# Four instead of five of sixteen chunk pairs multiplied in plain f32, with two elementwise steps moved to GpSimd

## The chip, the cores and the metric

The kernel runs on one core of one Trainium2 chip. The metric is the device time of one execution in microseconds (us). Of the three runs of the kernel before, the median is 2019.92 us (2019.54 to 2020.2).

## The reference

An attention through 49 agent tokens is followed by a two-layer network with the activation h - tanh(h). All tensors are float32; q, k and the agents are drawn eight times larger than in the function shown.

```python
B, N, C, n_agents, d_ff = 4, 12480, 128, 49, 2048
def sm(a, b):                                   # softmax of the scaled scores
    s = (a @ b.transpose(0, 2, 1)) / sqrt(C)
    e = exp(s - s.max(-1, keepdims=True))
    return e / (e.sum(-1, keepdims=True) + 1e-9)
agent_v = sm(agents, k) @ v                     # B x 49 x 128
x = (sm(q, agents) @ agent_v).reshape(B * N, C)
h = x @ w_in                                    # 49920 x 2048
out = (h - tanh(h)) @ w_out                     # 49920 x 128
```

## The kernel before

The 49920 tokens are worked through in 100 blocks of 500 (the last block of each batch has 480), and two blocks, an even and an odd one, make a pair that shares its load, its softmax and its store. A block goes through the 16 chunks of 128 hidden channels two at a time, so it has eight steps, and a pair has sixteen positions, 0 to 7 for the even block and 8 to 15 for the odd one. The agent values are multiplied into `w_in` beforehand, so that the first product needs only 49 rows.

One step, for 1000 values in each of 128 partitions, is this chain:

1. TensorE makes `h` in PSUM (`m1`, L563), 6 matmuls, split into high and low parts and run in the two row halves of the array side by side.
2. ScalarE makes `y` = tanh (L573) and `z` = the square of y, scaled (`square`, L578). For small h, h times this square is the wanted h - tanh(h).
3. VectorE makes `g` = h times z (`mul`, L583).
4. For a split position GpSimd rounds `g` to `gh` (`high`, L613) and VectorE makes the rest, `gl` = g - gh (`low`, L618). For a plain position, one in `PLAIN`, nothing is done.
5. TensorE adds the second product to `acc` (`m2`, L632): for a split position 12 matmuls in the reduced format (gh with both parts of `w_out`, then gl with its high part), for a plain position 4 matmuls in full f32 on `g`, with an f32 copy of the weights, `wo_f`. A row half of the array each.

In this text gh(6), gl(6), g(8) and so on are these instructions for the position in the brackets, and m2(6) is its second product.

The loop of `fast` (L850) writes the instructions in the order in which each engine then keeps them (`issue_order` pins it on VectorE, ScalarE, GpSimd and TensorE). At position k stand, in this order: g(k) and gh(k); the running side jobs; y(k+1) and z(k+1); h(k+2); gl(k-1); m2(k-1). At position 8 two `h` are made, h(10) and h(11), and none at 9. Two positions into a block the finished `acc` of the block before is drained: ScalarE copies one half (`take`, L644), VectorE adds the other (`add_up`, L641), and only then is its PSUM tile free for another `h`. PSUM holds four tiles of two banks in all, for `h`, `acc` and the side jobs.

Among the side jobs is the softmax of the next pair's queries (`q_softmax`). `QGAPS` sets how many positions lie between its parts: the scores on TensorE (L508), the maximum on VectorE (L515), at position 4 a subtraction on GpSimd (L517), an exponential on ScalarE (L519), then at position 9, behind g(9) on VectorE, the sum and the division (L521 to L527), and the low part on GpSimd (L529). In batches 0 to 2 the loop also carries the first attention of the next batch in small pieces; the last twelve pairs carry none.

Of the kernel before, what the change touches and what calls it, by code (L numbers as in the profile page):

```python
# [12 lines left out]
F32 = mybir.dt.float32  # L13
# [5 lines left out]
AF = mybir.ActivationFunctionType  # L19
ALU = mybir.AluOpType  # L20
# [3 lines left out]
B, N, C = 4, 12480, 128  # L24
# [28 lines left out]
GSC = float(np.sqrt(1.0 / (3.0 * 0.6)))  # L53
# [4 lines left out]
LATE = 3  # L58
KV = 3
VB = 4  # L60
PLAIN = (1, 3, 7, 8, 9)
NB = dict(y=2, z=2, g=4, gh=3, gl=3)
Q0 = 2
NV = 10
# [2 lines left out]
AHEADS = {8: (2, 3), 9: ()}  # L67
QL = 0
QS = 2
QGAPS = (1, 1, 0, 2, 3, 0, 0)  # L70
T0 = 11
T1 = 15
KS = {2: 1, 12: 2}
# [5 lines left out]
def width(n):  # L79
    return min(BLK, N - n % NBLK * BLK)  # L80


def column(n):
    return n // NBLK * N + n % NBLK * BLK
# [18 lines left out]
class Build:  # L103
# [31 lines left out]
    def constants(self):  # L135
# [17 lines left out]
        self.wo_l = c.tile([128, NCH, C], F32R, tag="wo_l", name="wo_l")  # L153
        self.wo_f = {i: c.tile([128, 2 * C], F32, tag=f"wo_f{i}", name=f"wo_f{i}") for i in sorted({i % 8 for i in PLAIN})}
        self.vb = [c.tile([128, GT, C + 2], F32, tag=f"v{i}", name=f"v{i}") for i in range(VB)]
# [52 lines left out]
    def split_w_out(self, c):  # L208
        nc = self.nc
        w = self.wf[:, c * 512 : (c + 1) * 512]  # L210
        h = self.wo_h[:, 4 * c : 4 * c + 4, :].rearrange("p n e -> p (n e)")
        l = self.wo_l[:, 4 * c : 4 * c + 4, :].rearrange("p n e -> p (n e)")
        nc.scalar.copy(h, w)
        nc.gpsimd.tensor_tensor(l, w, h.bitcast(F32), ALU.subtract)
        nc.gpsimd.memset(self.vb[c][:, :, C : C + 1], 1.0)
        for i, t in self.wo_f.items():
            if c == i // 2:
                nc.scalar.copy(t, w[:, 2 * C * (i % 2) :][:, : 2 * C])

    def phase1(self, b):  # L220
        nc = self.nc
# [351 lines left out]
        self.nc.scalar.activation(self.pair(y), h, AF.Tanh, scale=TSC)  # L573
        return y

    def square(self, y):
        z = self.wtile("z", NB["z"])[:, : y.shape[1]]
        self.nc.scalar.activation(z, y, AF.Square, scale=GSC)  # L578
        return z

    def mul(self, h, z, w):
# [31 lines left out]
        self.nc.gpsimd.tensor_scalar(gh, g, 1.0, 0.0, ALU.mult, ALU.add)  # L613
        return gh

    def low(self, g, gh):
        gl = self.wtile("gl", NB["gl"])[:, : g.shape[1]].bitcast(F32R)
        self.nc.vector.tensor_tensor(gl, g, gh.bitcast(F32), ALU.subtract)  # L618
        return gl

    def m2(self, acc, i, gh, gl, wf=None):
        nc = self.nc
        w = gh.shape[1] // 2
        high, low = (lambda c: self.wo_h[:, 2 * i + c, :]), (lambda c: self.wo_l[:, 2 * i + c, :])
        if gl is None:
            terms = [(lambda c: wf[:, c * C : (c + 1) * C], gh, c) for c in range(2)]
        else:
            terms = [(low, gh, 0), (high, gh, 0), (low, gh, 1), (high, gh, 1), (high, gl, 0), (high, gl, 1)]
        for k, (weights, g, c) in enumerate(terms):
            for r in range(2):  # L630
                rows = slice(HALF * r, HALF * (r + 1))
                nc.tensor.matmul(  # L632
                    acc[:, r, :w],
                    weights(c)[rows],
                    g[rows, c * w : (c + 1) * w],
                    start=i == 0 and k == 0,
                    stop=i == NCH // 2 - 1 and k == len(terms) - 1,
                )
# [46 lines left out]
    def fast(self):  # L685
        nc, tc = self.nc, self.tc
        HP = NCH // 2
        blocks = [(b, j) for b in range(B) for j in range(NBLK)]
        steps = [(n, i) for n in range(len(blocks)) for i in range(HP)]
# [7 lines left out]
        def q_job(p):  # L697
            pp[p] = []
            w = width(2 * p), width(2 * p + 1)
            halves = (blocks[2 * p][0], 0, w[0]), (blocks[2 * p + 1][0], w[0], w[1])  # L700
            return self.q_softmax(halves, qt.pop(p), pp[p], gaps=QGAPS if p > 1 else (1,) * 7)

# [88 lines left out]
        r1, r2, done = [], [], []  # L791
        acc, outs, hs, ys, zs = {}, {}, {}, {}, {}
# [6 lines left out]
        def out_at(n):  # L799
            first = n - n % 2  # L800
            if n == first and n // 2 not in outs:
                outs[n // 2] = self.work.tile([128, GW], F32, tag="out", name="o", bufs=2)
            return outs[n // 2][:, n % 2 * width(first) :][:, : width(n)]

        def finish(n):
            self.add_up(out_at(n), acc[n])
            if n % 2 == 1:
                w = width(n - 1) + width(n)
                nc.sync.dma_start(self.outT[:, column(n - 1) : column(n - 1) + w], outs[n // 2][:, :w])

# [5 lines left out]
        def tanhs(k):  # L816
            if k < len(steps):
                ys[k] = self.tanh(hs[k], width(steps[k][0]))

        def squares(k):  # L820
            if k < len(steps):
                zs[k] = self.square(ys.pop(k))

        def product(k):
            n, i = steps[k]
            g = self.mul(hs.pop(k), zs.pop(k), width(n))
            plain = n == 0 or n % 2 * HP + i in PLAIN
            gh = None if plain else self.high(g)
            r1.append((n, i, g, gh))

        def low(keep):
            while len(r1) > keep:
                n, i, g, gh = r1.pop(0)
                r2.append((n, i, g, None) if gh is None else (n, i, gh, self.low(g, gh)))

        def out(k):
            while r2:
                n, i, gh, gl = r2.pop(0)
                if i == 0:
                    acc[n] = self.banks("acc")  # L840
                wf = self.wf[:, 2 * C * i :] if n == 0 else self.wo_f.get(i)
                self.m2(acc[n], i, gh, gl, wf)
                if i == HP - 1:
                    done.append((n, k))

        for k in range(AHEAD):
            first_product(k)
        tanhs(0)
        squares(0)
        for k, (n, i) in enumerate(steps):  # L850
            b = blocks[n][0]
            pos = (n % 2) * HP + i
            p = n // 2
# [3 lines left out]
            if done and done[0][1] < k - 1:  # L857
                self.take(out_at(done[0][0]), acc[done[0][0]])
                finish(done.pop(0)[0])
            product(k)  # L860
            if n == LATE and i < NP:
                self.bound(0, i, slice(PCUT[i], PCUT[i + 1]))
# [15 lines left out]
            self.share(False)  # L878
            tanhs(k + 1)
            squares(k + 1)  # L880
            for j in AHEADS.get(pos, (AHEAD,)) if n else (AHEAD,):
                first_product(k + j)
            low(1)
            mark = self.last_on(ET.DVE)
            if n == 0:
# [6 lines left out]
            if pos in SPLIT and n < 2:  # L892
                first = self.count()
                self.split_w_out(SPLIT.index(pos))
                self.hold(first, mark, (ET.Activation, ET.Pool))
            out(k)
            if p and p + 1 < npair:
                if pos == QL:
# [4 lines left out]
            for kind in [x[0] for x in kq[:begin]]:  # L903
                if kind is kq[0][0] and kind.get(pos):
                    start(kq.pop(0)[1](pos))
        low(0)
        out(len(steps))
        while done:
            self.take(out_at(done[0][0]), acc[done[0][0]])
            finish(done.pop(0)[0])  # L910
# [64 lines left out]
```

## Time and profile before

| what | value |
|---|---|
| median of the runs | 2019.92 us |
| the profiled execution, its own time | 2023.43 us |
| its span, first to last instruction | 2021.6 us |
| mean granted TensorE clock | 0.994 |
| rounding `gh`, L613 on GpSimd | 545 instructions, 852.4 us busy |
| `gl`, L618 on VectorE | 545 instructions, 656.9 us busy |
| square `z`, L578 on ScalarE | 800 instructions, 831.4 us busy |
| plain second product, L632 with `wo_f` | 1976 matmuls |

Rows of the timeline give the start in us from the span's start, the duration in us, the engine, the line, the operation with its output and inputs, and in brackets how long the engine stood idle before it and what ended that. The duration of an instruction on VectorE is some 0.08 us longer than the distance to the next one behind it. Rows of the chain give the start, the length and the kind of work that the end of the program is followed back through.

### The profile page before, as it was taken

The numbers are of one execution on the slowest core, as the hardware profiler recorded it, in microseconds if no ns is written. First come the engines' busy times: TensorE is split into PE (matmuls) and PEld (weight loads), VectorE is DVE, ScalarE is ACT, GpSimd is POOL, SyncE is SP. The second block draws the span as 40 slices with busy tenths as digits, with TensorE's granted clock in tenths as the row PEclk, the third lists the DMA queues.
The fourth block names the chain that finished last, engine by engine and source line by source line (L and its number), as shares of the span: only waits on it lengthen the run. The fifth ranks groups of instructions, "written<-read, shape, count | busy, mean of one in ns | idle before, by whom it ended". The sixth has DMA issues, their size and how long they took to land.

```text
span 2021.6 us, 49580 instructions
## 1 busy us (share of the span) xinstructions
PE 1988.4 (98%) x20779; PEld 1462.1 (72%) x20779; DVE 1825.7 (90%) x1986; ACT 1806.5 (89%) x2052; POOL 999.0 (49%) x702
## 2 busy tenths in 40 slices
PE   8899999999999999999999999999999999999998
PEld 7477767777777777777677777777766777777776
DVE  7799899889999998998999999889899989999997
ACT  3689998899989998889999999898999999999997
POOL 1154455555444545555454454555545556555554
PEclk9899999999999999999999999999999999999999
DMA  9322212221121222222012111221101111101100
GB/s 346 116 83 78 74 41 85 85 61 44 44 71 61 78 74 61 65 77 71 29 35 91 64 58 43 71 61 56 53 30 34 45 38 33 54 29 37 39 24 27
DMA packets 76601, 129.70 MB, mean 64 GB/s; under 512 B 5384, under 2 KB 55376, under 8 KB 76368
## 3 DMA queue, kind: packets, MB, share of 16 engines
q1 hardware_dynamic: 76368, 126.44, 19.1%
q8 instruction: 165, 2.70, 0.5%
q14 instruction: 68, 0.56, 0.1%
HBM read 81.10 MB, written 25.56 MB: 53 GB/s over the span
## 4 chain that ended last, share of the span: by engine, by line
PE 83%; ACT 9%; DVE 6%; issue 1%; DMA 0%; POOL 0%; SPq 0%; DVEq 0%; POOLq 0%
PE acc L632 48%; PE h L563 26%; ACT z L578 4%; ACT y L573 4%; DVE g L583 3%; PE misc L508 2%; PE misc L357 2%; PE pt L538 1%; PE misc L301 1%; DVE gl L618 1%; PE h L273 1%; PE misc L472 1%; ACT s L349 0%; DVE qe L524 0%; DVE qs L521 0%
## 5 line engine op out<-in xcount | busy, mean ns | idle before, releaser
L613 POOL TENSOR_SCALAR gh<-g 128x1000 fp32r<-128x1000 f32 (+1 forms) x545 | 852.4, 1564 | 621.0 <-DVE g L583 583.0
L583 DVE TENSOR_TENSOR g<-h,z 128x1000 f32<-128x1000 f32 (+1 forms) x800 | 954.4, 1193 | 134.3 <-ACT z L578 123.6
L573 ACT ACTIVATE y<-h 128x1000 f32<-128x1000 f32 (+1 forms) x800 | 802.4, 1003 | 68.7 <-PE h L563 60.8
L578 ACT ACTIVATE z<-y 128x1000 f32<-128x1000 f32 (+1 forms) x800 | 831.4, 1039 | 25.4
L618 DVE TENSOR_TENSOR gl<-g,gh 128x1000 fp32r<-128x1000 f32 (+1 forms) x545 | 656.9, 1205 | 1.2 <-POOL gh L613 0.9
L563 PE MATMUL h<-pT,awh 49*128 49x504 f32 x1600 | 554.2, 425 | 0.0
L632 PE MATMUL acc<-g,wo_f 64*128 64x500 f32 (+1 forms) x1976 | 447.1, 578 | 0.1
L632 PE MATMUL acc<-gh,wo_l 64*128 64x500 f32 (+1 forms) x2180 | 432.9, 387 | 0.4 <-POOL gh L613 0.2
L632 PE MATMUL acc<-gh,wo_h 64*128 64x500 f32 (+1 forms) x2180 | 432.8, 386 | 0.0
L563 PE MATMUL h<-pT,awl 49*128 49x504 f32 x800 | 369.9, 462 | 9.4 <-DVE g L583 4.6
L632 PE MATMUL acc<-gl,wo_h 64*128 64x500 f32 (+1 forms) x2180 | 341.2, 387 | 1.6 <-DVE gl L618 0.9
L563 PE MATMUL h<-pb,awh 49*128 49x504 f32 x1600 | 317.9, 388 | 0.0
L563 PE MATMUL h<-pb,awl 49*128 49x504 f32 x800 | 309.7, 387 | 0.0
L632 PEld LDWEIGHTS acc<-g,wo_f 64*128 64x128 f32 x1976 | 192.3, 186 | 147.0 <-issue 129.1
L563 PEld LDWEIGHTS h<-pT,awh 49*128 49x128 f32 x1600 | 266.9, 186 | 20.4 <-issue 10.7
L632 PEld LDWEIGHTS acc<-gh,wo_h 64*128 64x128 f32 x2180 | 214.4, 186 | 37.2
L632 PEld LDWEIGHTS acc<-gl,wo_h 64*128 64x128 f32 x2180 | 211.3, 184 | 41.4 <-DVE gl L618 7.3
L632 PEld LDWEIGHTS acc<-gh,wo_l 64*128 64x128 f32 x2180 | 211.3, 184 | 38.3 <-POOL gh L613 1.7
L563 PEld LDWEIGHTS h<-pT,awl 49*128 49x128 f32 x800 | 147.8, 185 | 118.3 <-DVE o L641 50.9
L529 POOL TENSOR_TENSOR pp<-qe,pp 128x392 fp32r<-128x392 f32 x50 | 51.5, 1029 | 265.4 <-DVE pp L527 257.3
L563 PEld LDWEIGHTS h<-pb,awh 49*128 49x128 f32 x1600 | 154.8, 185 | 29.3
L563 PEld LDWEIGHTS h<-pb,awl 49*128 49x128 f32 x800 | 149.7, 187 | 14.1 <-issue 7.7
(113 smaller groups left out, 1123.2 us busy)
## 6 DMA issues: line engine op xcount, KB each, us to landing
kt<-kT SPq DMA_DIRECT2D x48, 512.0 KB
qt<-qT SPq DMA_DIRECT2D x46, 500.0 KB
outT<-o SPq DMA_DIRECT2D x46, 500.0 KB
pb<-pT SPq DMA_DIRECT2D x200, 96.5 KB
v<-v SPq DMA_DIRECT2D x36, 512.0 KB
vt<-v SPq DMA_DIRECT2D x12, 512.0 KB
raw<-w_in SPq DMA_DIRECT2D x4, 512.0 KB
v<-w_out SPq DMA_DIRECT2D x4, 512.0 KB
```

The lines of the kernel that those rows point to most:

```text
L273: nc.tensor.matmul(ps[:, t // 4, (t % 4) * A2 : (t % 4 + 1) * A2], kt[:, t, :], self.ag[:, 0:2, :], start=True, stop=True,)
L301: nc.tensor.matmul(to, kt[:, t, r : r + QUART], self.ag[:, b, :], start=True, stop=True)
L357: nc.tensor.matmul(ps[HALF * odd : HALF * odd + w, : C + 1], flat[:r, t * A : t * A + w], vt[:r, t, : C + 1], start=t < 2, stop=t >= n - 2,)
L508: nc.tensor.matmul(to, qt[:, token : token + QUART], self.ag[:, b, :], start=True, stop=True)
L529: nc.gpsimd.tensor_tensor(pp[:, :, HALF:PW], ev, pp[:, :, :A].bitcast(F32), ALU.subtract)
L563: nc.tensor.matmul(h[:, c, : BT * TT], aw[a][rows[c], sl], pT[p][rows[c], :], start=k == 0, stop=k == 2)
L573: self.nc.scalar.activation(self.pair(y), h, AF.Tanh, scale=TSC)
L578: self.nc.scalar.activation(z, y, AF.Square, scale=GSC)
L583: self.nc.vector.tensor_tensor(self.pair(g), h, self.pair(z), ALU.mult)
L613: self.nc.gpsimd.tensor_scalar(gh, g, 1.0, 0.0, ALU.mult, ALU.add)
L618: self.nc.vector.tensor_tensor(gl, g, gh.bitcast(F32), ALU.subtract)
L632: nc.tensor.matmul(acc[:, r, :w], weights(c)[rows], g[rows, c * w : (c + 1) * w], start=i == 0 and k == 0, stop=i == NCH // 2 - 1 and k == ...
```

## The change

Position 3 leaves the list of plain positions: its product is now split, with gh(3) made by GpSimd and, unlike all others, gl(3) too. From block 2 on the square of position 8 is made by GpSimd as y times y, with the scale put into the weights instead (`wo_f` of chunk pair 0). In the queries' softmax the exponential moves one position later. The last step of all is plain, and the last two blocks are stored by a transfer each.

```diff
-PLAIN = (1, 3, 7, 8, 9)
+PLAIN = (1, 7, 8, 9)
+POOL_LOW = (3,)
+POOL_SQ = (8,)
...
-QGAPS = (1, 1, 0, 2, 3, 0, 0)
+QGAPS = (1, 1, 0, 3, 2, 0, 0)
...
     def square(self, y, pool=False):
         z = self.wtile("z", NB["z"])[:, : y.shape[1]]
+        if pool:
+            self.nc.gpsimd.tensor_tensor(z, y, y, ALU.mult)
+        else:
+            self.nc.scalar.activation(z, y, AF.Square, scale=GSC)
         return z
...
     def low(self, g, gh, pool=False):
         gl = self.wtile("gl", NB["gl"])[:, : g.shape[1]].bitcast(F32R)
-        self.nc.vector.tensor_tensor(gl, g, gh.bitcast(F32), ALU.subtract)
+        (self.nc.gpsimd if pool else self.nc.vector).tensor_tensor(gl, g, gh.bitcast(F32), ALU.subtract)
         return gl
...
         def finish(n):
             self.add_up(out_at(n), acc[n])
-            if n % 2 == 1:
+            if n >= len(blocks) - 2:
+                nc.sync.dma_start(self.outT[:, column(n) : column(n) + width(n)], out_at(n))
+            elif n % 2 == 1:
...
+        def by_pool(k):
+            return steps[k][0] > 1 and position(k) in POOL_SQ
...
         def product(k):
             n, i = steps[k]
             g = self.mul(hs.pop(k), zs.pop(k), width(n))
-            plain = n == 0 or n % 2 * HP + i in PLAIN
+            plain = n == 0 or position(k) in PLAIN or k == len(steps) - 1
             gh = None if plain else self.high(g)
+            gl = self.low(g, gh, True) if gh is not None and position(k) in POOL_LOW else None
```

GpSimd, one of the last pairs, positions 2 to 9, before. The `gh` are those of positions 2, 4, 5 and 6, `qe` is the softmax's subtraction and `pp` its low part:

```order
L613 TENSOR_SCALAR gh_24075<-g_24073 128x1000
L613 TENSOR_SCALAR gh_24154<-g_24152 128x1000
L517 TENSOR_TENSOR qe_24157<-qe_24157,qm_24156 128x392
L613 TENSOR_SCALAR gh_24179<-g_24177 128x1000
L613 TENSOR_SCALAR gh_24208<-g_24206 128x1000
L529 TENSOR_TENSOR pp_97<-qe_24157,pp_97 128x8x49
```

The same with the change:

```order
L619 TENSOR_SCALAR gh_24589<-g_24587 128x1000
L619 TENSOR_SCALAR gh_24608<-g_24606 128x1000
L624 TENSOR_TENSOR gl_24610<-g_24606,gh_24608 128x1000
L619 TENSOR_SCALAR gh_24672<-g_24670 128x1000
L520 TENSOR_TENSOR qe_24675<-qe_24675,qm_24674 128x392
L619 TENSOR_SCALAR gh_24705<-g_24703 128x1000
L619 TENSOR_SCALAR gh_24734<-g_24732 128x1000
L582 TENSOR_TENSOR z_24766<-y_24764 128x1000
L532 TENSOR_TENSOR pp_96<-qe_24675,pp_96 128x8x49
```

Three instructions of 1000 values came in: gh(3) and gl(3) ahead of gh(4), and the square of position 8 directly behind gh(6).

ScalarE at the same place, before. The second row is the exponential, followed by y and z of positions 7, 8 and 9 and the half of `acc` that ScalarE copies:

```order
L578 ACTIVATE z_24183<-y_24181 128x1000
L519 ACTIVATE qe_24157<-qe_24157 128x392
L573 ACTIVATE y_24211<-h_24185 128x1000
L578 ACTIVATE z_24213<-y_24211 128x1000
L573 ACTIVATE y_24238<-h_24215 128x1000
L578 ACTIVATE z_24240<-y_24238 128x1000
L573 ACTIVATE y_24265<-h_24242 128x1000
L578 ACTIVATE z_24267<-y_24265 128x1000
```

The same with the change:

```order
L584 ACTIVATE z_24709<-y_24707 128x1000
L576 ACTIVATE y_24736<-h_24711 128x1000
L584 ACTIVATE z_24738<-y_24736 128x1000
L522 ACTIVATE qe_24675<-qe_24675 128x392
L576 ACTIVATE y_24764<-h_24740 128x1000
L576 ACTIVATE y_24791<-h_24768 128x1000
L584 ACTIVATE z_24793<-y_24791 128x1000
```

The exponential now stands ahead of y(8) instead of y(7), and behind y(8) the square is gone. The order on VectorE at this place has the same instructions in the same order as before:

```order
L624 TENSOR_TENSOR gl_24747<-g_24703,gh_24705 128x1000
L589 TENSOR_TENSOR g_24761<-h_24711,z_24738 128x1000
L624 TENSOR_TENSOR gl_24775<-g_24732,gh_24734 128x1000
L589 TENSOR_TENSOR g_24789<-h_24740,z_24766 128x1000
L589 TENSOR_TENSOR g_24813<-h_24768,z_24793 128x1000
L524 TENSOR_REDUCE qs_24676<-qe_24675 128x8
```

These are gl(5), g(7), gl(6), g(8), g(9) and the softmax's sum; only the maker of z(8), which g(8) reads, is another.

More of the change, by code (lines that the diff above doesn't have):

```diff
@@ L217, in split_w_out @@
             if c == i // 2:
-                nc.scalar.copy(t, w[:, 2 * C * (i % 2) :][:, : 2 * C])
+                scale = GSC * GSC if i in {p % 8 for p in POOL_SQ} else 1.0
+                nc.scalar.mul(t, w[:, 2 * C * (i % 2) :][:, : 2 * C], scale)
     def phase1(self, b):
@@ L574, in tanh, with square @@
         return y
-    def square(self, y):
+    def square(self, y, pool=False):
         z = self.wtile("z", NB["z"])[:, : y.shape[1]]
-        self.nc.scalar.activation(z, y, AF.Square, scale=GSC)
+        if pool:
+            self.nc.gpsimd.tensor_tensor(z, y, y, ALU.mult)
+        else:
+            self.nc.scalar.activation(z, y, AF.Square, scale=GSC)
         return z
@@ L614, in high, with low @@
         return gh
-    def low(self, g, gh):
+    def low(self, g, gh, pool=False):
         gl = self.wtile("gl", NB["gl"])[:, : g.shape[1]].bitcast(F32R)
-        self.nc.vector.tensor_tensor(gl, g, gh.bitcast(F32), ALU.subtract)
+        (self.nc.gpsimd if pool else self.nc.vector).tensor_tensor(gl, g, gh.bitcast(F32), ALU.subtract)
         return gl
@@ L818, in tanhs, with position @@
                 ys[k] = self.tanh(hs[k], width(steps[k][0]))
+        def position(k):
+            n, i = steps[k]
+            return n % 2 * HP + i
+        def by_pool(k):
+            return steps[k][0] > 1 and position(k) in POOL_SQ
         def squares(k):
             if k < len(steps):
-                zs[k] = self.square(ys.pop(k))
+                zs[k] = self.square(ys.pop(k), by_pool(k))
         def product(k):
@@ L826, in product @@
             g = self.mul(hs.pop(k), zs.pop(k), width(n))
-            plain = n == 0 or n % 2 * HP + i in PLAIN
+            plain = n == 0 or position(k) in PLAIN or k == len(steps) - 1
             gh = None if plain else self.high(g)
-            r1.append((n, i, g, gh))
+            gl = self.low(g, gh, True) if gh is not None and position(k) in POOL_LOW else None
+            r1.append((n, i, g, gh, gl))
         def low(keep):
             while len(r1) > keep:
-                n, i, g, gh = r1.pop(0)
-                r2.append((n, i, g, None) if gh is None else (n, i, gh, self.low(g, gh)))
+                n, i, g, gh, gl = r1.pop(0)
+                r2.append((n, i, g, None) if gh is None else (n, i, gh, gl or self.low(g, gh)))
         def out(k):
@@ L840, in out @@
                     acc[n] = self.banks("acc")
-                wf = self.wf[:, 2 * C * i :] if n == 0 else self.wo_f.get(i)
+                wf = self.wf[:, 2 * C * i :] if n < 2 else self.wo_f.get(i)
                 self.m2(acc[n], i, gh, gl, wf)
```

## The prediction

> **What bounds the kernel now.** I read the busy shares first, then the chain of waits, then the timeline of each engine in one pair.
>
> ```profile
> span 2021.6 us, 49580 instructions
> PE 1988.4 (98%) x20779; PEld 1462.1 (72%) x20779; DVE 1825.7 (90%) x1986; ACT 1806.5 (89%) x2052; POOL 999.0 (49%) x702
> PE 83%; ACT 9%; DVE 6%; issue 1%; DMA 0%; POOL 0%; SPq 0%; DVEq 0%; POOLq 0%
> ```
>
> The second line gives busy us and share of each engine, the third the shares of the chain. TensorE is busy nearly all of the span and carries 83% of the chain; VectorE and ScalarE follow closely, and only GpSimd is half idle. So a microsecond that TensorE loses in a pair is lost for good, and one that it saves counts only if nobody makes it wait further on. The chain in one of the last pairs, from h(6) to h(12):
>
> ```profile
> 1728.60 0.69 PE h L563 x6
> 1729.29 1.68 PE acc L632 x8
> 1730.97 0.69 PE h L563 x6
> 1731.66 1.37 PE acc L632 x12
> ...
> 1735.77 1.36 PE acc L632 x12
> 1737.13 1.36 PE h L563 x12
> 1738.49 3.36 PE acc L632 x16
> 1741.84 0.76 PE h L563 x4
> ```
>
> These are h(6), the plain m2(3), h(7), the split m2(4), then m2(6), h(10) with h(11), m2(7) with m2(8), and h(12). TensorE has no gap. A plain product takes 1.68 us, a split one 1.37 us. The other engines at the same place:
>
> ```profile
> 1725.26 1.19 DVE L618 TENSOR_TENSOR gl<-g,gh 128x1000 fp32r<-128x1000 f32 x1
> 1729.39 1.20 DVE L583 TENSOR_TENSOR g<-h,z 128x1000 f32<-128x1000 f32 x1 [1.37 <-ACT z L578]
> 1730.51 1.19 DVE L618 TENSOR_TENSOR gl<-g,gh 128x1000 fp32r<-128x1000 f32 x1
> 1734.95 1.19 DVE L618 TENSOR_TENSOR gl<-g,gh 128x1000 fp32r<-128x1000 f32 x1
> 1736.05 1.19 DVE L583 TENSOR_TENSOR g<-h,z 128x1000 f32<-128x1000 f32 x1
> 1737.92 1.20 DVE L583 TENSOR_TENSOR g<-h,z 128x1000 f32<-128x1000 f32 x1 [0.68 <-ACT z L578]
> 1739.04 0.55 DVE L521 TENSOR_REDUCE qs<-qe 128x8 f32<-128x392 f32 x1
> 1740.95 0.67 DVE L641 TENSOR_TENSOR o<-o,acc 128x500 f32<-128x500 f32 x1
> ```
>
> ```profile
> 1727.71 1.03 POOL L613 TENSOR_SCALAR gh<-g 128x1000 fp32r<-128x1000 f32 x1 [2.55 <-DVE g L583]
> 1728.72 0.83 POOL L517 TENSOR_TENSOR qe<-qe,qm 128x392 f32<-128x392 f32 x1
> 1730.75 1.84 POOL L613 TENSOR_SCALAR gh<-g 128x1000 fp32r<-128x1000 f32 x1 [1.20 <-DVE g L583]
> 1732.96 1.84 POOL L613 TENSOR_SCALAR gh<-g 128x1000 fp32r<-128x1000 f32 x1 [0.37 <-DVE g L583]
> 1733.76 1.01 ACT L573 ACTIVATE y<-h 128x1000 f32<-128x1000 f32 x1
> 1734.80 1.04 ACT L578 ACTIVATE z<-y 128x1000 f32<-128x1000 f32 x1
> ```
>
> On VectorE these are gl(2), g(5), gl(4), gl(6), g(8), g(9), the softmax's sum and the draining of the old `acc`; on GpSimd gh(4), the softmax's subtraction, gh(5) and gh(6); on ScalarE y(8) and z(8). The drain ends at 1741.62, just before h(12) takes its PSUM tile at 1741.84: position 8 to 10 has no slack on either path.
>
> The rounding on GpSimd takes 1.03 us when nothing stands beside it and 1.84 us behind a `gl`: gh(5) ends at 1732.59, 0.89 us behind gl(4), which ended at 1731.70. It works the other way round too:
>
> ```profile
> 307.08 1.03 POOL L613 TENSOR_SCALAR gh<-g 128x1000 fp32r<-128x1000 f32 x1 [0.41 <-DVE g L583]
> 307.34 1.82 DVE L618 TENSOR_TENSOR gl<-g,gh 128x1000 fp32r<-128x1000 f32 x1
> 101.37 1.29 POOL L214 TENSOR_TENSOR wo_l<-awh,wo_h 128x512 fp32r<-128x512 f32 x1
> 101.53 2.18 DVE L618 TENSOR_TENSOR gl<-g,gh 128x1000 fp32r<-128x1000 f32 x1
> L618 DVE TENSOR_TENSOR gl<-g,gh x545: 1137/1190/2181, 99.3 to 2011.6; 128x1000 fp32r<-128x1000 f32 x175, 128x960 fp32r<-128x960 f32 x7
> ```
>
> A `gl` that starts while GpSimd is at work ends 1.05 us behind GpSimd's end (309.16 against 308.11; 103.71 against 102.66). Of the two, whoever starts second waits for the whole of the first. `g`, which reads h from PSUM, is not slowed: 1.20 us at 1729.39, 1.19 us at 1736.05.
>
> **The change part by part.** There are 49 pairs that it touches (all but the first): twelve last ones without side jobs, and 37 with them.
>
> *The split of position 3.* TensorE saves 1.68 - 1.37 = 0.31 us a pair, 15 us in all, if gh(3) and gl(3) are there in time.
>
> *GpSimd's two long instructions.* No row shows a two-input one of 1000 values. The nearest are:
>
> ```profile
> L517 POOL TENSOR_TENSOR qe<-qe,qm 128x392 f32<-128x392 f32 x50 | 42.5, 849 | 41.8 <-DVE qm L515 41.8
> L214 POOL TENSOR_TENSOR wo_l<-awh,wo_h 128x512 fp32r<-128x512 f32 x4 | 5.1, 1281 | 36.9 <-ACT wo_h L213 36.9
> ```
>
> Scaled by their size, the first gives 849 / 392 x 1000 = 2.17 us, the second 2.50 us. From below the one-input rounding bounds it, 1.03 us. I take 2.17, since that row has f32 in and out as the square has.
>
> *The walk through one of the last pairs.* gh(3) waits for gl(2), which ends at 1726.45, and ends at about 1727.48; gl(3) on GpSimd runs to 1729.65, beside g(4) and an idle VectorE, so it costs nothing itself, and m2(3) at 1729.29 wants it only 0.9 us into its run. But gh(4) now runs to 1730.68 and the subtraction directly behind it to 1731.51. gl(4) could start at 1730.71 and finds GpSimd at work; it ends at 1732.56 instead of 1731.70. VectorE is full from there on, 1.11 us from start to start: gl(5) 1733.59 to 1734.78, gh(6) behind it to 1735.67, and gl(6) could start at 1735.81. y(8) ends at 1734.77. The moved exponential does not alter that, since it went from before y(7) to before y(8) and ScalarE is full. So the square starts at once behind gh(6), at 1735.67, 0.14 us ahead of gl(6), and runs to 1737.84. gl(6) ends 1.05 us later, at 1738.89. The last four matmuls of m2(6), a third of 1.37 us, end at 1739.34 instead of 1737.13. h(10) follows to 1740.02, h(11) needs the tile that g(8) has read (1738.81 to 1740.00) and is not held further. With m2(7) and m2(8), h(12) starts at 1744.06 instead of 1741.84: 2.2 us lost, the saving of 0.31 already in it. VectorE's drain, behind g(8), g(9) and the softmax's 1.9 us, ends at about 1743.6 and is not what holds h(12). On GpSimd the softmax's low part is queued behind the square, but waits for VectorE longer anyway. Twelve such pairs: 26.4 us.
>
> *The pairs with side jobs.* TensorE takes longer there, and GpSimd's backlog is gone before position 6. In one with two score jobs:
>
> ```profile
> 1194.39 1.85 POOL L613 TENSOR_SCALAR gh<-g 128x1000 fp32r<-128x1000 f32 x1 [0.37 <-DVE g L583]
> 1195.19 1.01 ACT L573 ACTIVATE y<-h 128x1000 f32<-128x1000 f32 x1
> 1196.38 1.19 DVE L618 TENSOR_TENSOR gl<-g,gh 128x1000 fp32r<-128x1000 f32 x1
> 1198.56 1.36 PE h L563 x12
> ```
>
> gh(6) ends at 1196.24 and y(8) at 1196.20, so the square runs from 1196.25 to 1198.42, ahead of gl(6) by 0.13 us. gl(6) ends at 1199.47 and m2(6) at 1199.92, where before h(10) started at 1198.56: 1.36 us lost. I take it for all 37: 50.3 us.
>
> *ScalarE* is spared 1.04 us a pair. It is nowhere waited for after that, since g(9) now waits for g(8) and not for z(9): worth nothing.
>
> *The end.* The last product goes without gh and gl:
>
> ```profile
> 2010.79 0.71 PE L632 MATMUL acc<-gl,wo_h 64*128 64x480 f32 x4
> 2012.84 0.71 PE L632 MATMUL acc<-gl,wo_h 64*128 64x480 f32 x4
> ```
>
> m2(14) ends at 2011.50 and the last one at 2013.55. In f32 it needs 1.68 x 480 / 500 = 1.61 us behind the former: 2013.11, a gain of 0.4 us. The last store is half as large; I put 0.4 us on that, between nothing and the same again.
>
> *The sum.* 26.4 + 50.3 - 0.8 = 75.9 us on an execution of 2023.43 us (span 2021.6 and 1.83 us around it): 2099.3. The median of the runs lies 3.51 us below that execution, so I forecast 2095.8 us.
>
> **A rule weighed against the rows.** The square and gl(6) meet in every pair, and the sum hangs on the one waiting for the whole of the other, as the rows at 101 and 307 us have it. [...] By the rule the sum is the 2096 above; if a long GpSimd instruction let gl through, it would be the 2040 of the third rival.
>
> **The rivals.**
>
> 1. *gl(6) gets in first* (the leads of 0.13 and 0.14 us are small). Then the square follows it, and g(8) comes later still: in the score pair the square ends at 1197.57 + 2.03 (0.14 us of it done while it waits, as with gh(5)), g(8) at 1200.82, h(11) at 1201.50 and h(12), with the 3.36 us of m2(7) and m2(8), at 1204.86 instead of 1203.28, 1.6 us lost; in a last pair 2.5 us. 37 x 1.6 + 12 x 2.5 - 0.8 = 88: 2108 us.
> 2. *Faster: the square is short enough.* h(12) comes 0.31 us early if g(8) has ended by 1198.93 in the score pair, so if the square takes 1.45 us or less and leaves gl(6) alone. A square of one tile with itself at the rounding's 1.03 us would do. Then 49 x 0.31 + 0.8 = 16 us are gained: 2004 us. Against it: two-input rows of 392 values take 849 ns already, and the rounding holds `gl` up as well.
> 3. *No holding, but 2.17 us.* z(8) lands at 1198.42, g(8) ends at 1199.65, h(11) at 1200.33, h(12) at 1203.69: 0.4 us lost a pair, 20 us: 2040 us. Against it stand the two pairs of rows above.
> 4. *A wash:* the square in between these, gain and loss within 0.2% (4 us, what a measurement of this kernel can tell from no change).
>
> **How the numbers follow.** The forecast 0.64, the rivals 0.10, 0.10, 0.11 and 0.05 in their order. With 2.50 us instead of 2.17 the forecast's case reaches 2114, the first rival 2126; so its own range is 2075 to 2126. To leave out no more than 2 in 10, the range reaches down over the third rival: 2033 to 2130. Slower by over 0.2%: 0.64 + 0.10 + 0.11 = 0.85; faster 0.10; the same 0.05.
>
> **What would show it.** In the profile after: GpSimd's square and gl(3) at about 2.2 us each; gl(6) in most pairs at some 3.2 us instead of 1.19, with the square's end 1.05 us before its own; TensorE waiting some 2 us a pair in front of the last four matmuls of m2(6), put down to VectorE's `gl`; TensorE's busy share down from 98% to about 95%; each of the last pairs some 2 us longer. A square of 1.5 us or less, or a `gl` of 1.19 us beside it, would prove me wrong, as would a PSUM tile that h(11) gets without waiting for g(8).

## The result and the profile after

The changed kernel takes 2101.58 us, the median of 4 runs (2100.41 to 2102.58), against 2020.06 us before, in 4 runs beside it. The ratio is 1.0403 with a 95% interval of 1.0391 to 1.0415: 81.5 us slower. The profiled execution took 2102.58 us. Its page, with the span, the engines' busy shares and the shares of the chain of waits:

```profile
span 2100.7 us, 50058 instructions
PE 1992.0 (95%) x20971; PEld 1470.3 (70%) x20971; DVE 1900.8 (90%) x1985; ACT 1759.0 (84%) x2002; POOL 1307.5 (62%) x848
PE 57%; DVE 22%; ACT 11%; POOL 5%; issue 4%; DMA 0%; SPq 0%; POOLq 0%; DVEq 0%
```

TensorE is busy for 1992.0 us, about as long as before (1988.4), but the span has grown by 79 us: TensorE waits. Its share of the chain has fallen from 83% to 57%, and VectorE's has risen from 6% to 22%.

To see where, the softmax's subtraction serves as a clock, since there is one a pair. The timeline's row eleven from the end and the last one, before and then after:

```profile
1581.23 0.84 POOL L517 TENSOR_TENSOR qe<-qe,qm 128x392 f32<-128x392 f32 x1
1949.86 0.84 POOL L517 TENSOR_TENSOR qe<-qe,qm 128x392 f32<-128x392 f32 x1
```

```profile
1635.89 0.86 POOL L520 TENSOR_TENSOR qe<-qe,qm 128x392 f32<-128x392 f32 x1
2026.84 0.84 POOL L520 TENSOR_TENSOR qe<-qe,qm 128x392 f32<-128x392 f32 x1
```

Ten periods of 36.86 us have become ten of 39.10 us, 2.23 us more in each. The 37 periods ahead of them, with side jobs and the first two of the last twelve pairs, have grown by 1.50 us in the mean. Together that is 77.8 us of the 79. Inside one of the last pairs the timeline after shows this on GpSimd (gl(3), the softmax's subtraction, gh(6), the square), VectorE (gl(4), gl(6)) and TensorE (the last four matmuls of m2(4) and of m2(6)):

```profile
1788.95 2.36 POOL L624 TENSOR_TENSOR gl<-g,gh 128x1000 fp32r<-128x1000 f32 x1
...
1792.28 0.83 POOL L520 TENSOR_TENSOR qe<-qe,qm 128x392 f32<-128x392 f32 x1
...
1795.46 1.81 POOL L619 TENSOR_SCALAR gh<-g 128x1000 fp32r<-128x1000 f32 x1 [0.40 <-DVE g L589]
1797.24 1.85 POOL L582 TENSOR_TENSOR z<-y 128x1000 f32<-128x1000 f32 x1
...
1792.34 1.83 DVE L624 TENSOR_TENSOR gl<-g,gh 128x1000 fp32r<-128x1000 f32 x1 [0.22 <-POOL gh L619]
...
1797.42 2.73 DVE L624 TENSOR_TENSOR gl<-g,gh 128x1000 fp32r<-128x1000 f32 x1
...
1794.22 0.73 PE L638 MATMUL acc<-gl,wo_h 64*128 64x500 f32 x4 [0.45 <-DVE gl L624]
...
1800.20 0.72 PE L638 MATMUL acc<-gl,wo_h 64*128 64x500 f32 x4 [1.46 <-DVE gl L624]
```

The square starts directly behind gh(6) and 0.18 us ahead of gl(6). It runs to 1799.09, and gl(6) ends at 1800.15, 1.06 us behind it: the whole `gl` is done after the square. TensorE stands still for 1.46 us in front of the last four matmuls of m2(6). The other held `gl` is gl(4), behind the subtraction, and costs 0.45 us in front of m2(4)'s last four. The waits of the whole run, before and after, in us, times and the longest:

```profile
PEld acc L632 <- DVE gl L618: 7.3, 17, 0.9
```

```profile
PEld acc L638 <- DVE gl L624: 101.9, 106, 1.9
PE acc L638 <- DVE gl L624: 63.6, 61, 1.5
```

TensorE's weight loads and its matmuls are listed apart and overlap (70% and 95% of the span), so the two lines are not to be added. Both point to `gl`, for which TensorE hardly waited before.

### The profile page after: what moved, and what is told of

Its sections match the earlier page's. It is cut to its first block, busy times and chain, and to the rows that moved or that the text cites. A ratio compares the mean times of both kernels' runs of the same rounds, so it can differ in the third digit from the quotient of the medians.

```text
span 2100.7 us, 50058 instructions
## 1 busy us (share of the span) xinstructions
PE 1992.0 (95%) x20971; PEld 1470.3 (70%) x20971; DVE 1900.8 (90%) x1985; ACT 1759.0 (84%) x2002; POOL 1307.5 (62%) x848
## 4 chain that ended last, share of the span: by engine, by line
PE 57%; DVE 22%; ACT 11%; POOL 5%; issue 4%; DMA 0%; SPq 0%; POOLq 0%; DVEq 0%
PE acc L638 32%; PE h L566 18%; DVE g L589 9%; DVE gl L624 9%; ACT y L576 5%; ACT z L584 5%; POOL gh L619 2%; POOL gl L624 2%; PE misc L360 2%; PE misc L511 1%; PE pt L541 1%; PE misc L304 1%; PE h L276 1%; POOL z L582 1%; PE misc L475 1%
## 5 line engine op out<-in xcount | busy, mean ns | idle before, releaser
L619 POOL TENSOR_SCALAR gh<-g 128x1000 fp32r<-128x1000 f32 (+1 forms) x593 | 948.9, 1600 | 450.4 <-DVE g L589 413.0
L584 ACT ACTIVATE z<-y 128x1000 f32<-128x1000 f32 (+1 forms) x751 | 780.4, 1039 | 25.6 <-DVE g L589 2.0
L624 DVE TENSOR_TENSOR gl<-g,gh 128x1000 fp32r<-128x1000 f32 (+1 forms) x544 | 731.4, 1345 | 5.2 <-POOL gh L619 5.1
L638 PE MATMUL acc<-gh,wo_l 64*128 64x500 f32 (+1 forms) x2372 | 472.9, 387 | 0.3 <-POOL gh L619 0.2
L638 PE MATMUL acc<-gh,wo_h 64*128 64x500 f32 (+1 forms) x2372 | 472.0, 386 | 0.0
L638 PE MATMUL acc<-gl,wo_h 64*128 64x500 f32 (+1 forms) x2372 | 380.4, 395 | 64.6 <-DVE gl L624 63.6
L638 PE MATMUL acc<-g,wo_f 64*128 64x500 f32 (+1 forms) x1576 | 356.1, 580 | 0.0
L638 PEld LDWEIGHTS acc<-gh,wo_h 64*128 64x128 f32 x2372 | 234.4, 186 | 39.1 <-issue 0.5
L638 PEld LDWEIGHTS acc<-gh,wo_l 64*128 64x128 f32 x2372 | 231.3, 184 | 39.9 <-POOL gh L619 1.1
L638 PEld LDWEIGHTS acc<-g,wo_f 64*128 64x128 f32 x1576 | 153.4, 187 | 122.2 <-issue 104.8
```

The costliest lines, as they stand in the source:

```text
L624: (self.nc.gpsimd if pool else self.nc.vector).tensor_tensor(gl, g, gh.bitcast(F32), ALU.subtract)
L638: nc.tensor.matmul(acc[:, r, :w], weights(c)[rows], g[rows, c * w : (c + 1) * w], start=i == 0 and k == 0, stop=i == NCH // 2 - 1 and k == ...
```

## The experiments

In the edits the kernel that each starts from is named. Times of the kernel before, in the same series, are 2019.3 to 2019.7 us. The period of the last pairs is the median of ten; the score pairs are three neighbouring pairs that each carry two side jobs of attention scores, and theirs is the median too.

| kernel | median us | ratio, 95% interval | period of last pairs | of score pairs |
|---|---|---|---|---|
| before | 2020.06 | 1 | 36.87 | 39.22 |
| changed | 2101.58 | 1.0391 to 1.0415 | 39.10 | 40.81 |
| square alone | 2085.14 | 1.0304 to 1.0336 | 38.19 | 40.61 |
| square back | 2031.32 | 1.0040 to 1.0068 | 37.55 | 39.24 |
| six plain, square | 2034.82 | 1.0057 to 1.0088 | 37.16 | 39.57 |
| six plain | 2025.77 | 1.0018 to 1.0037 | 37.03 | 39.57 |
| four plain | 2017.78 | 0.9986 to 1.0004 | 36.89 | 39.41 |
| old gaps | 2029.38 | 1.0036 to 1.0064 | 37.53 | 39.23 |
| later subtraction | 2042.81 | 1.0104 to 1.0135 | 37.72 | 39.53 |
| end alone | 2020.63 | 0.9997 to 1.0015 | 36.87 | 39.28 |
| square dropped | 2021.94 | 1.0002 to 1.0020 | 36.94 | 39.32 |
| gl(6) first | 2168.13 | 1.0726 to 1.0759 | 41.29 | 41.38 |

**Square back.** The changed kernel with the square on ScalarE again.

```diff
-POOL_SQ = (8,)
+POOL_SQ = ()
```

> The changed kernel with only the square of position 8 back on ScalarE; gl(3) on GpSimd, four plain positions, the later exponential and the new end stay. Theory (the square is the loss: it holds gl(6) up): nearly the whole loss goes; 49 x 0.31 us saved on TensorE less some 0.5 us in each of the last twelve pairs, where the subtraction behind gh(4) still holds gl(4): about 2012 us (2006 to 2020). Rival (GpSimd's gl(3), 2.36 us, and its backlog carry the loss): 2060 us or more.

It took 2031.32 us: 70 of the 81.5 us go with the square. The remainder is some 19 us larger than expected, so the time misses the expected range.

**Square alone.** The kernel before, with nothing of the change but the square.

```diff
+POOL_SQ = (8,)
...
+        def by_pool(k):
+            return steps[k][0] > 1 and position(k) in POOL_SQ
...
-                zs[k] = self.square(ys.pop(k))
+                zs[k] = self.square(ys.pop(k), by_pool(k))
```

> The kernel before with only the square of position 8 moved to GpSimd; five plain positions, old exponential, old end. Theory (whoever starts second waits for the whole other one): the square of 1.86 us starts behind gh(6), 0.14 us ahead of gl(6), which ends 1.05 us behind it; 1.1 us lost a pair, 49 pairs: about 2072 us (2060 to 2085). Rival A (only z(8) comes later, gl(6) isn't held in effect): 0.1 us a pair, about 2026 us. Rival B (gl(3) on GpSimd is needed for the loss): within 5 us of 2020.

2085.14 us: 65.4 us lost by this one instruction a pair, 1.33 us each where 1.1 was expected, so the time lies at the upper edge of the expected range. Its timeline in a last pair, on GpSimd and on VectorE:

```profile
1709.44 1.85 POOL L582 TENSOR_TENSOR z<-y 128x1000 f32<-128x1000 f32 x1
...
1709.54 2.81 DVE L624 TENSOR_TENSOR gl<-g,gh 128x1000 fp32r<-128x1000 f32 x1
```

With a lead of 0.10 us the square holds gl(6) to 1712.35, again 1.06 us behind its own end. The rivals without holding fall. By medians the parts nearly add up: 65.4 for the square and 11.6 for the rest make 77.0 of 81.5 us.

**Six plain, with the square and without.** From the kernel before, position 6 is plain instead of position 3, so that no gl(6) meets the square; the second kernel is the control.

```diff
-PLAIN = (1, 3, 7, 8, 9)
+PLAIN = (1, 6, 7, 8, 9)
+POOL_SQ = (8,)
```

In the control the last line is `POOL_SQ = ()`.

> Plain positions 1, 6, 7, 8, 9 instead of 1, 3, 7, 8, 9, so that there is no gl(6) behind which or ahead of which the square could stand; the square of position 8 on GpSimd; gl(3) on VectorE; old exponential and end. To be read against the next run, the same with the square on ScalarE. Theory (the loss is gl(6) and the square excluding each other): with no gl(6), z(8) is late but g(8) still comes in time for h(11): within 8 us of the next run. Rival A (a late z(8) is the loss by itself): 40 us or more above it.

> The control to the run before: plain positions 1, 6, 7, 8, 9, the square of position 8 on ScalarE, all else as in the kernel before. As many plain and split products as before, so about 2020 us by both theories (2010 to 2035, as gl(3) now meets the fuller VectorE at position 4).

The square now costs 9.1 us (2034.82 against 2025.77), 0.18 us a pair, instead of 65.4. That is just over the 8 us expected and far from the rival's 40. In the profile with the square, the timeline of the same place and then the chain:

```profile
1704.75 1.85 POOL L582 TENSOR_TENSOR z<-y 128x1000 f32<-128x1000 f32 x1 [1.89 <-ACT y L576]
...
1706.64 2.42 DVE L589 TENSOR_TENSOR g<-h,z 128x1000 f32<-128x1000 f32 x2 [1.35 <-POOL z L582]
```

```profile
1705.64 1.68 PE acc L638 x8
1707.32 1.52 PE h L566 x12
```

VectorE is idle for 1.35 us in front of g(8), and yet the path loses only 0.16 us, in h(10) and h(11), which took 1.36 together before. So it is not the late z(8) by itself but the `gl` held behind the square that costs.

**Square dropped.** From the kernel with the square alone. It leaves the square of position 8 out of the computation; g(8) takes y(8) in its place.

```diff
-                zs[k] = self.square(ys.pop(k), by_pool(k))
+                zs[k] = ys.pop(k) if by_pool(k) else self.square(ys.pop(k))
```

> The kernel before without the square of position 8 on any engine from block 2 on: y itself is used as z there, so that part of the computation is left out. It shows what ScalarE's relief of 1.04 us a pair is worth when nothing is paid for it. Theory (TensorE bounds, the relief is worth next to nothing): 2010 to 2021 us. Rival (ScalarE's unbroken run from y(5) to z(9), which the chain follows in some pairs, bounds them): 49 x 0.3 to 1.04 us less, 1969 to 2005 us.

2021.94 us, no gain, and just above the expected range: taking 1.04 us a pair off ScalarE is worth nothing. The interval even has the kernel 0.4 to 4.0 us slower than the one before, and why is open. VectorE's timeline, g(8) with y for z, and g(9):

```profile
1735.66 1.19 DVE L589 TENSOR_TENSOR g<-h,y 128x1000 f32<-128x1000 f32 x1
1737.59 1.20 DVE L589 TENSOR_TENSOR g<-h,z 128x1000 f32<-128x1000 f32 x1 [0.74 <-ACT z L584]
```

g(9) still waits for z(9), since h(9), and so y(9), comes when TensorE makes it.

**Four plain.** The changed kernel with both steps back on VectorE and ScalarE, so that the split of position 3 and the new end remain.

```diff
-POOL_LOW = (3,)
-POOL_SQ = (8,)
-QGAPS = (1, 1, 0, 3, 2, 0, 0)
+POOL_LOW = ()
+POOL_SQ = ()
+QGAPS = (1, 1, 0, 2, 3, 0, 0)
```

> Four plain positions and the new end, with gl(3) on VectorE and every square on ScalarE, the old exponential: the change without GpSimd's two new instructions. Theory (TensorE bounds the pair, and VectorE, idle for 1.37 us in front of g(5), has room for a gl of 1.11 us there): most of 49 x 0.31 us is gained: about 2007 us (2002 to 2016). Rival (VectorE becomes the bound with one more gl a pair): 2020 us or more. The other theory of the loss in the run with the square back on ScalarE (2031 us) was GpSimd's gl(3) and the backlog behind it; then this run must lie some 20 us below it.

A miss: 2017.78 us, with 1 inside the interval. The 15 us that TensorE saves are nearly all gone. The chain, m2(4), m2(5) and m2(6) in a last pair:

```profile
1725.92 1.44 PE acc L638 x11
...
1728.05 1.54 PE acc L638 x11
...
1730.28 1.52 PE acc L638 x12
```

Before, each took 1.36 or 1.37. The 0.08, 0.17 and 0.16 us make 0.41, against 0.31 saved. From gl(3) at 1722.53 to the end of g(8) at 1732.14 VectorE's timeline has no gap; before, it stood idle for 1.37 us in front of g(5), the place that a plain position 3 leaves. Two things fill it. A split position takes VectorE 2 x 1.11 = 2.22 us and TensorE 0.69 + 1.37 = 2.06, so with five of them in a row VectorE falls behind by 0.16 us at each. And gl(3) itself is held. GpSimd's gh(4), then gl(3) and g(5) on VectorE:

```profile
1722.30 1.03 POOL L619 TENSOR_SCALAR gh<-g 128x1000 fp32r<-128x1000 f32 x1 [0.38 <-DVE g L589]
...
1722.53 1.84 DVE L624 TENSOR_TENSOR gl<-g,gh 128x1000 fp32r<-128x1000 f32 x1
1724.30 1.19 DVE L589 TENSOR_TENSOR g<-h,z 128x1000 f32<-128x1000 f32 x1
```

gl(3) starts 0.23 us behind gh(4) and ends 1.04 us behind its end, so it takes the 1.77 us up to g(5) and not the 1.11 for which there was room. The z(5) that g(5) reads is there at 1723.94. By an estimate from these rows, g(5) could have started 0.34 us earlier without the hold, and most of the 0.41 would not have been lost; no run takes the hold away.

**Old gaps, and a later subtraction.** Two kernels on what was left over with the square back: the exponential at its old place, and the subtraction behind gh(5).

```diff
-POOL_SQ = (8,)
-QGAPS = (1, 1, 0, 3, 2, 0, 0)
+POOL_SQ = ()
+QGAPS = (1, 1, 0, 2, 3, 0, 0)
```

> The changed kernel with the square back on ScalarE and the softmax's exponential back at its old place, one position earlier; gl(3) stays on GpSimd. It tells what holds the last 11 us of the kernel with the square back (2031.3 us). Theory: GpSimd's backlog. gl(3) takes it 2.36 us, gh(4) follows, and the subtraction behind it holds gl(4); the exponential has no part in it: 2031 us (2027 to 2035), last pairs still 37.5 us. Rival: the moved exponential delays y(8) and with it g(8): then the time falls back to 2018 to 2022 us, last pairs 36.9 us.

```diff
-POOL_SQ = (8,)
-QGAPS = (1, 1, 0, 3, 2, 0, 0)
+POOL_SQ = ()
+QGAPS = (1, 1, 1, 2, 2, 0, 0)
```

> The changed kernel with the square back on ScalarE and the softmax's subtraction on GpSimd one position later, behind gh(5) instead of gh(4). Theory: what holds gl(4) is that GpSimd is late behind gl(3), whatever comes next in its queue. g(5) has ended by 0.2 us before gh(4) does, so gh(5) takes the subtraction's place, starts ahead of gl(4), and holds it for 1.03 us instead of 0.85: no gain, 2031 to 2038 us, gl(4) in the last pairs still 1.8 us or more. Rival: the subtraction itself is what costs; out of the way, gl(4) takes 1.19 us, and the time falls to 2018 to 2025 us.

The moved exponential is not it: 2029.38 us and the same periods. The later subtraction makes it worse, as GpSimd's backlog would, but by more than expected, 2042.81 us. The timeline in a last pair: GpSimd with gh(4) and gh(5) in one row, and VectorE's gl(4).

```profile
1700.57 2.36 POOL L624 TENSOR_TENSOR gl<-g,gh 128x1000 fp32r<-128x1000 f32 x1
1702.89 2.04 POOL L619 TENSOR_SCALAR gh<-g 128x1000 fp32r<-128x1000 f32 x2
...
1703.96 2.01 DVE L624 TENSOR_TENSOR gl<-g,gh 128x1000 fp32r<-128x1000 f32 x1 [0.22 <-POOL gh L619]
```

Here gl(4) is held by gh(5), which follows gh(4), as it was by the subtraction before. In the last pairs that costs 0.17 us over the kernel with the square back, as expected; what I had left out is that the score pairs then lose 0.29 us each too, where the subtraction had cost nothing (39.24 against 39.22 before).

**End alone.** From the kernel before, the new end.

```diff
-            if n % 2 == 1:
+            if n >= len(blocks) - 2:
+                nc.sync.dma_start(self.outT[:, column(n) : column(n) + width(n)], out_at(n))
+            elif n % 2 == 1:
...
-            plain = n == 0 or n % 2 * HP + i in PLAIN
+            plain = n == 0 or position(k) in PLAIN or k == len(steps) - 1
```

> The kernel before with the new end alone: last product plain, last two blocks stored by a transfer each. Theory: 0.4 us for the missing gh and gl and 0.4 us for the smaller last transfer: 0.8 us less than before (0.3 to 1.5). Rival: no part of it, within 0.3 us.

2020.63 us against 2019.66. The interval reaches from 0.6 us less to 3.0 us more, so no gain is seen, and the expected 0.8 us lie just outside it.

**gl(6) first.** The changed kernel, with GpSimd's square made to wait for gl(6).

```diff
-            squares(k + 1)
+            later = k + 1 < len(steps) and by_pool(k + 1)
+            if not later:
+                squares(k + 1)
...
+            if later:
+                first = self.count()
+                squares(k + 1)
+                self.wait_for(first, self.last_on(ET.DVE))
```

> The changed kernel with the square of position 8 made to wait for gl(6), so that gl(6) is never held up and the square comes behind it. Theory (the first rival of the prediction: g(8) and with it h(11) come later instead): 0 to 0.4 us a pair worse than the changed kernel, 2100 to 2122 us. Rival (only the holding of gl(6) costs): m2(6) is on time again and most of the loss goes, 2060 us or less.

2168.13 us, beyond every theory. The timeline in a last pair, the square and h(11), and the chain behind them:

```profile
1805.64 1.85 POOL L582 TENSOR_TENSOR z<-y 128x1000 f32<-128x1000 f32 x1 [1.47 <-DVE gl L624]
...
1808.79 0.49 PE L566 MATMUL h<-pT,awl 49*128 49x504 f32 x1 [1.82 <-DVE g L589]
```

```profile
1808.79 0.95 PE h L566 x6
1809.74 5.05 PE acc L638 x16
1814.79 0.69 PE h L566 x6
```

The stall of 1.82 us in front of h(11), which waits for g(8), was expected of the first rival. Then m2(7) and m2(8) take 5.05 us instead of 3.36, and that was not. The last section shows why. Eight of the ten last pairs have this slow stretch. Where it is missing, the period of a last pair is 39.62 us, 0.5 more than in the changed kernel, where 0 to 0.4 was expected.

## Why the prediction was right

The forecast was 2095.8 us, 5.8 below the median, and its mechanism is the one that the runs show. Point by point:

- **Whoever starts second waits for the whole of the first.** Shown three ways: gl(6) at 2.73 us, its end 1.06 us behind the square's, where 1.05 was forecast; the square alone at 65.4 us; and 9.1 us where no gl(6) is near. The row at 1736.05 that the prediction gives for `g` not being slowed has no GpSimd instruction beside it. A row that has one bears it out: g(7) of the kernel before, at 1733.83, takes 1.20 us beside gh(6) (1732.96 to 1734.80). None of the 800 `g` takes more than 1.22 us in the kernel before, or more than 1.21 in the changed one.
- **Who starts first.** Forecast: the square, by 0.14 us. Measured: by 0.18 us in the last pair shown. In 36 of 49 pairs gl(6) takes 2.67 to 2.87 us; in 6 with other VectorE work in between it starts later in the square and takes 1.74; in 7 gl(6) takes 1.14 to 1.19 and the square waits, 2.9 to 3.2 us, though its row starts 0.03 to 0.33 us ahead. In 6 of these 7 that start falls into a reduction on VectorE of 0.67 us (L487), in the other into the last 0.12 us of g(6); what lets gl(6) in there was not tried.
- **The length of the square.** Mis-sized: 2.17 us taken, 1.85 measured where nothing holds it. gl(3) went the other way, 2.36 instead of 2.17: two-input instructions of one size differ by 0.5 us. The shorter one has a single tile as both inputs and writes f32 instead of fp32r; which of the two makes it shorter was not tried. So gl(6) took 2.73 us where some 3.2 had been named, and TensorE stood 1.46 us in front of m2(6)'s last four matmuls where some 2 had.

```profile
L582 POOL TENSOR_TENSOR z<-y 128x1000 f32<-128x1000 f32 x47 | 87.1, 1853 | 109.8 <-ACT y L576 107.8 <-DVE gl L624 2.1
```

  (This group is that of six plain with the square, busy us and mean ns behind the bar.)
- **The last pairs.** Forecast 2.2 us, measured 2.23, by two errors that cancel. Counted from gl(2)'s end, gl(6) ended after 12.18 us (forecast 12.44, the shorter square), but the last four matmuls of m2(6) took 0.72 us from start to end behind a stall. The forecast had 0.45, a third of 1.37, which is what they add to the chain when they run close behind other matmuls: in the kernel before they start at 1736.51 and the next `h` at 1736.96. That the size came out is luck. The hold on gl(4), forecast in the walk, is there.
- **The number of pairs.** Ten lose 2.2 us, not twelve: the first two lost 1.31 and 1.41, as those with side jobs.
- **The pairs with side jobs.** Forecast 1.36 us, measured 1.50. The square alone costs the score pairs 1.39 and the square back 0.02; the whole change 1.59. That the two together cost 0.2 more than their sum stays unexplained.
- **The split of position 3.** Here the step was wrong in what it says of the saving: "if gh(3) and gl(3) are there in time" gave 15 us. With `gl` on VectorE it comes to nothing that can be told (four plain), because VectorE has no gap from gl(3) to g(8), in part since gh(4) holds gl(3). With gl(3) on GpSimd 10 to 12 us are lost (old gaps, square back). GpSimd's backlog holds gl(4) there, 1.83 us instead of 1.19 in the last pairs; that this is the whole loss is argued from the timelines, not shown. "It costs nothing itself" holds for m2(3), not for what comes behind. In the forecast's walk the loss was hidden in that of gl(6), so the sum did not suffer.
- **ScalarE's relief is worth nothing:** shown by the square dropped.
- **The end.** Forecast -0.8 us. The product itself came out as worked out. TensorE's timeline after:

```profile
2091.32 0.70 PE L638 MATMUL acc<-gl,wo_h 64*128 64x480 f32 x4
2091.86 1.77 PE L638 MATMUL acc<-g,wo_f 64*128 64x480 f32 x8
```

  The last product ends 1.61 us behind m2(14) (2093.63 against 2092.02), where it took 2.05 before. From there to the end of the span it is 7.07 us after, 8.05 before and 9.49 in the kernel with the end alone, so what the smaller store brings is lost in that spread, and no run shows the 0.4 us that I put on it.

The first rival (gl(6) first, 2108 us) had the order of events of that case right, and where the order was forced the time was 60 us above it, some 39 of them by the clock (last section). The second (1.45 us or less) falls with the square's 1.85 us, the third (no holding) with the square alone, and the fourth (a wash) with the 81.5 us.

## What to carry to other kernels

Before work is moved to an idle GpSimd, look at what VectorE does at that very moment: in the changed kernel a square on GpSimd that started 0.04 to 0.18 us ahead of a `gl` on the critical path held it, in 36 of 49 pairs, until 1.04 to 1.07 us behind its own end. By themselves the 49 squares, 1.85 us each where nothing holds them, cost 65 us, while beside a stretch without a `gl` they cost 9. What is saved on the busiest engine counts only up to the next one: compare the steps' lengths over the stretch (here 2.22 us on VectorE against 2.06 on TensorE), not the busy shares of the whole run, and fill an idle place by what the instruction will take there (gl(3): 1.84 us, not 1.19). And a forecast that comes out right is to be taken apart all the same; this one held in part by errors that cancelled.

## What the hardware showed that was not expected

Behind a stall of 1.82 us TensorE was granted half its clock for 3.40 us. The stretches of the kernel with gl(6) first around the stall shown above; behind the busy times of the engines stand the granted clock (1 is full speed), the DMA share and GB/s:

```profile
1806.97:1808.79 1.82, 0.00 (x1) 0.01 (x2) 1.26 (x2) 1.00 (x1) 0.53 (x1) 1.00 0.00 0
1808.79:1809.75 0.96, 0.96 (x8) 0.85 (x10) 0.96 (x1) 0.93 (x1) 0.00 (x0) 1.00 0.00 0
1809.75:1813.15 3.40, 3.40 (x10) 1.38 (x10) 1.86 (x6) 0.29 (x2) 1.02 (x1) 0.50 0.00 0
```

TensorE stalls for 1.82 us, works at full speed for 0.96 us, and then gets half the clock for 3.40 us, in which it loses half, 1.70 us: the 5.05 us instead of 3.36. Of the 49 such stalls in this run 23 are followed by a stretch of half the clock, and 23 x 1.70 us make 39 us. The mean clock says the same: it is 0.978 against 0.996 in the changed kernel, (0.996 - 0.978) x 2164.8 = 39 us, which is most of the 46 us by which the time passed the expected range.

The length of the stall does not tell which: it is 1.73 to 2.01 us in the 23, and 1.62 to 2.02 us in the 26 that are spared. Its place tells more. All changes of the granted clock in this trace lie on one grid of 3.41 us, to within 2 ns. Here are two steps of that grid around a spared stall (1767.33 to 1769.16) and two around the stall shown above:

```profile
1765.40:1768.81 3.41, 1.93 (x16) 1.05 (x12) 1.37 (x2) 2.77 (x3) 1.86 (x1) 1.00 0.00 0
1768.81:1772.22 3.41, 3.06 (x18) 1.82 (x20) 3.17 (x7) 1.52 (x3) 0.02 (x1) 1.00 0.02 5
1806.36:1809.77 3.41, 1.59 (x14) 1.05 (x12) 2.24 (x3) 2.50 (x3) 1.14 (x1) 1.00 0.00 0
1809.77:1813.18 3.41, 3.41 (x10) 1.36 (x9) 1.84 (x6) 0.30 (x2) 1.02 (x1) 0.50 0.00 0
```

A border of the grid, at 1768.81, cuts the spared stall, and 1.48 us of it fall into one step; the other lies in one step with all of its 1.82 us. Over the 49 stalls, the fullest step of the 23 holds 1.64 to 2.01 us of idle time, and that of the 26 spared ones 0.81 to 1.67, so in this run the two part at about half a step, 1.64 to 1.67 of 3.41 us. In the changed kernel, whose stalls in front of m2(6) last up to 1.53 us, it happens once between its start and its end, at 544 us (a clock of 0.50 from 544.56 to 547.96), behind a stall of 1.50 us; so the idle time in a step does not settle it alone, and what else does is open.
